# The last token block in three stores, and one batch's input loads ten steps later

## The chip, the cores and the metric

The kernel runs on one core of a Trainium2 chip. Its time is device microseconds, the median of several executions. A profile of one execution is read beside it: busy times of the engines, waits between them, DMA transfers. The engines are named as there: PE is TensorE (matmuls; PEld its weight loads), ACT is ScalarE, DVE is VectorE, POOL is GpSimd, and SP is the engine that issues most DMAs.

## The reference, cut to what matters

```python
X = np.fft.rfft(x, axis=1)                  # x: 8 x 3008 x 256
y = np.fft.irfft(X * (filt_r + 1j * filt_i)[None], n=3008, axis=1)
h = y.reshape(24064, 256) @ w_in            # 256 x 2048
g = h / (1 + np.exp(-beta * h))             # beta: one value per column
out = g @ w_out                             # 2048 x 256, float32
```

A filter over the sequence in the frequency domain, and then two dense layers with a Swish between them.

## The kernel before, in words

**The two halves.** The transform of one batch is cut into four stages of small matmuls: s1 (line 572), s2 (588, followed by the filter's multiplications on VectorE and one addition, yh, on POOL, 607), s3 (617) and s4 (639). Between s1 and s2, and between s3 and s4, the data goes through DRAM to be rearranged: stores `d<-a` and loads `a<-d` (lines 352 and 580, called a2 loads here), stores `d<-z` and loads `zz<-d` (623 and 628). The input rows come by `load_x`, four DMAs of 384 KB per batch, which POOL issues (line 171)[...].

The dense layers go over 47 blocks of 512 tokens, each in 16 steps, one per 128 columns of the hidden layer; 752 steps in all. In step s two matmuls per piece of tokens put the hidden columns into `hps` (line 726), a PSUM tile with two buffers. ScalarE reads it, applies the Swish and writes `gT` (line 735), 128 x 512 in bfloat16. Two steps later, four matmuls (line 746) multiply it with `wout_sb` and add to `acc`, one matmul for each group of 128 tokens. `acc` is two PSUM tiles per block, each of two groups, out of a pool of three. After step 16 of a block both are copied to `ost` and stored.

**What sets the order.** The program's order is written out by hand, and each engine runs its instructions in that order. Batch 0 is transformed ahead of the steps, with all engines. Batch b's transform is spread over the steps in which batch b-1's tokens go through the dense layers: `at(step, function, ...)` puts a piece of work into a table `plan`, and each step runs, in this order, its two hidden matmuls and Swish, the pieces that the table has for it, and the four output matmuls of two steps before. For batch 1, whose base step is 0, s1 is at steps 0 to 7, the a2 loads at step 10, s2 at steps 19 to 46 and s3 five steps after each s2; the second batch's (index 1) z stores follow every third s3. s1 of the third batch (index 2) starts at step 54. The four x loads of the third batch are at steps 14, 17, 20 and 23; POOL issues them between its other work, SP issues the a2 loads, z stores and output stores.

**The end.** The last block is handled like the others, but its two `acc` tiles are copied by ScalarE and VectorE at once, and stored by two DMAs of SP, 256 KB each (line 762); other blocks are copied by VectorE twice and stored by one DMA of 512 KB (line 764).

Of the kernel before, what the change touches and what calls it, by code (L numbers as in the profile page):

```python
# [10 lines left out]
P = 128  # L11
# [4 lines left out]
F32 = mybir.dt.float32  # L16
# [20 lines left out]
def kernel(  # L37
# [10 lines left out]
    nc = tc.nc  # L48

    B, S, D = x.shape  # L50
# [6 lines left out]
    NFB = FF // P  # L57
    NP = 2 * N1
    KP = 4 * NK
    TB = 512  # L60
    assert TOK % TB == 0
    NBLK = TOK // TB
    NSTEP = NBLK * NFB
# [7 lines left out]
    tw = dict(reuse_waits="tile")  # L71
# [31 lines left out]
    wout_sb = wpool.tile([P, NFB, D], BF16, name="wout_sb", tag="wout_sb")  # L103
# [6 lines left out]
    def evac(dst, src, on_act, scale=None):  # L110
        if on_act:
            nc.scalar.activation(dst, src, ACT.Copy, scale=1.0 if scale is None else scale)  # L112
        elif scale is None:
            nc.vector.tensor_copy(dst, src)  # L114
        else:
            nc.vector.tensor_scalar_mul(dst, src, scale)  # L116
# [439 lines left out]
    hpsum = ctx.enter_context(tc.tile_pool(name="hpsum", bufs=2, space=bass.MemoryType.PSUM, **tw))  # L556
    opsum = ctx.enter_context(tc.tile_pool(name="opsum", bufs=3, space=bass.MemoryType.PSUM, **tw))
    fpsum = ctx.enter_context(tc.tile_pool(name="fpsum", bufs=3, space=bass.MemoryType.PSUM, **tw))
    gpool = ctx.enter_context(tc.tile_pool(name="gpool", bufs=4, **tw))
    a2pool = ctx.enter_context(tc.tile_pool(name="a2pool", bufs=5, **tw))  # L560
    zpool = ctx.enter_context(tc.tile_pool(name="zpool", bufs=2, **tw))
    zzpool = ctx.enter_context(tc.tile_pool(name="zzpool", bufs=4, **tw))
# [2 lines left out]
    ostp = ctx.enter_context(tc.tile_pool(name="ostp", bufs=2, **tw))  # L565
# [86 lines left out]
    def at(s, fn, *a):  # L652
        plan.setdefault(int(s), []).append((fn, a))

    def s1_steps(b, units_, steps, act, on_act=()):
        assert len(steps) == len(units_)
        for i, s in zip(units_, steps):
            at(s, s1, b, i, i in on_act)
            if i % 4 == 3:
                at(s, a1_store, b, i // 4)  # L660

    def s23_steps(b, steps, lag, act):
        assert len(steps) == NU
        for i, s in enumerate(steps):
            at(s, s2, b, i)
            at(s + lag, s3, b, i, i % act == act - 1 if act else False)

    def s4_steps(b, steps, act):
        assert len(steps) == J // 4 * NDC
        for i, s in enumerate(steps):  # L670
            at(s, s4, b, i, i % act == act - 1 if act else False)

    for b in range(1, B):
        o = first_step[b - 1]
        if b == 1:
            s1_steps(1, range(16), [o + i // 2 for i in range(16)], False, range(1, 16, 2))
            for g in range(NG):
                at(o + 10, a2_load, 1, g)
            s23_steps(1, [o + r for r in (19, 21, 23, 26, 28, 30, 34, 36, 39, 41, 44, 46)], 5, 1)
            for h in range(J // JG):  # L680
                at(o + 56, zz_load, 1, h)
            s4_steps(1, [o + 67 + (i * 12) // 15 for i in range(16)], 2)
            for f in (2, 3):
                at(f, load_wout, f * WG)
                at(f, scale_wout, f * WG)
            if B > 2:
                for g in range(4):
                    at(o + 14 + 3 * g, load_x, 2, g)
                late = (54, 55, 56, 57, 58, 59, 60, 61, 66, 67, 68, 70, 72, 73, 74, 76)
                s1_steps(2, range(16), [o + r for r in late], False)  # L690
                for g in range(NG):
                    at(o + 80, a2_load, 2, g)
                if B > 3:
                    for g in range(4):
                        at(o + (62, 68, 88, 92)[g], load_x, 3, g)
            continue
        base = [o + 16 * n + s for n in range(4) for s in (4, 8, 12)]
        if b == 2:
            base[:6] = [o + r for r in (8, 12, 19, 22, 26, 29)]
        s23_steps(b, base, 6, False)  # L700
        for h in range(J // JG):
            at(o + 70, zz_load, b, h)
        s4_steps(b, [o + 80 + (i * 13) // 15 for i in range(16)], False)
        if b + 1 < B:
            early = [o + 16 * n + s for n in range(4) for s in (7, 13)]
            late = [o + s for s in (66, 67, 69, 70, 72, 73, 75, 76)]
            s1_steps(b + 1, range(16), early + late, False)
            for g in range(NG):
                at(o + 82, a2_load, b + 1, g)
            if b + 2 < B:  # L710
                for g in range(4):
                    at(o + (30, 62, 88, 92)[g], load_x, b + 2, g)

    blk = {}
    LAG = 2
    for s in range(NSTEP + LAG):
        if s < NSTEP:
            i, fb = divmod(s, NFB)
            t0 = i * TB
            hps = hpsum.tile([P, TB], F32, name="hps", tag="hps")  # L720
            pos = t0
            while pos < t0 + TB:
                b, n0 = divmod(pos, S)
                ln = min(S - n0, t0 + TB - pos)
                for dc in range(NDC):
                    nc.tensor.matmul(  # L726
                        hps[:, pos - t0 : pos - t0 + ln],
                        lhsT=win_sb[:, dc, fb * P : (fb + 1) * P],
                        rhs=ys[b][:, dc, n0 : n0 + ln],
                        start=(dc == 0),  # L730
                        stop=(dc == NDC - 1),
                    )
                pos += ln
            gT = gpool.tile([P, TB], BF16, name="gT", tag="gT")
            nc.scalar.activation(gT[:], hps[:], ACT.Silu, scale=beta_sb[:, fb : fb + 1])  # L735
            blk[s] = gT
        for fn, a in plan.get(s, ()):
            fn(*a)
        if s >= LAG:
            i, fb = divmod(s - LAG, NFB)  # L740
            t0 = i * TB
            gT = blk.pop(s - LAG)
            if fb == 0:
                acc = [opsum.tile([P, 2, D], F32, name="acc", tag="acc") for _ in range(2)]
            for tb in range(4):
                nc.tensor.matmul(  # L746
                    acc[tb // 2][:, tb % 2, :],
                    lhsT=gT[:, tb * P : (tb + 1) * P],
                    rhs=wout_sb[:, fb, :],
                    start=(fb == 0 and tb % 2 == 0),  # L750
                    stop=(fb == NFB - 1),
                    skip_group_check=True,
                )
            if fb == NFB - 1:
                ost = ostp.tile([P, 4, D], F32, name="ost", tag="ost")
                rows = out[t0 : t0 + TB, :].rearrange("(c p) d -> p c d", p=P)
                last = s == NSTEP + LAG - 1
                for h in range(2):
                    hs = slice(2 * h, 2 * h + 2)
                    evac(ost[:, hs, :], acc[h][:], last and h == 0)  # L760
                    if last:
                        nc.sync.dma_start(rows[:, hs, :], ost[:, hs, :])
                if not last:
                    nc.sync.dma_start(rows, ost[:])


# [1 line left out]
_INS = ['x', 'filt_r', 'filt_i', 'moe_w_in', 'moe_w_out', 'moe_beta']  # L768
_OUTS = [((24064, 256), 'float32')]
# [25 lines left out]
```

## Time and profile before

| what | value |
|---|---|
| median of 5 runs (785.72 to 787.02) | 786.1 us |
| the profiled execution | 786.1 us |
| its span, first to last instruction | 784.0 us |
| TensorE busy | 764.6 us |
| ScalarE busy | 559.3 us |
| VectorE busy | 437.9 us |
| POOL busy | 151.4 us |
| mean granted TensorE clock | 0.998 |
| output stores of the last block: issue to landing, least and most | 2.1 and 2.4 us |
| a2 loads: least, median and most | 3.1, 5.1 and 9.7 us |

Times within the span count from its first instruction. A row of the timeline gives the start, the duration, the engine, the line and operation, what is written and read, and in brackets how long the engine stood idle before it and what released it. Matmuls are pipelined: one of 256 columns shows 0.27 us, but they follow each other every 0.108, so starts are compared, not durations. The chain is the work that ended last, followed back from the last instruction to whatever released each piece.

### The profile page before, as it was taken

Reading aid. Unit: us, or ns where it says so; the run is one execution under the profiler, and the core shown is the slowest. Engines: PE = TensorE matmul, PEld = TensorE weight load, DVE = VectorE, ACT = ScalarE, POOL = GpSimd, SP = SyncE. Lnnn points to the kernel's source line nnn. Section 1 sums busy time; section 2 is a strip of 40 time slices with the busy share of each in tenths; the row PEclk is TensorE's granted clock in tenths of the full one; section 3 lists DMA queues with packets and bytes.
Section 4 is the critical chain, followed back from the end, with each engine's and each line's share of the span. In section 5 each row is a group of like instructions: output and inputs, shape, how many; then the busy total and the mean of one; then the engine's idle time right before and its main releaser. Section 6 shows DMA issues by size and latency. Waiting matters only on the chain.

```text
span 784.0 us, 15166 instructions
## 1 busy us (share of the span) xinstructions
PE 764.6 (98%) x5978; PEld 545.0 (70%) x6071; DVE 437.9 (56%) x681; ACT 559.3 (71%) x824; POOL 151.4 (19%) x160
## 2 busy tenths in 40 slices
PE   8799999999999999999999999999999999999997
PEld 5666667766677667866678666776667766676664
DVE  8747754776556665566656675566655666321001
ACT  7787867676677766777667766677766777777775
POOL 6724300322012120122101222012200222000000
PEclk9999999999999999999999999999999999999999
DMA  9968385234922349133580416612164111500101
GB/s 175 227 184 189 101 205 166 68 88 120 240 72 65 98 114 255 35 85 98 122 235 29 130 52 166 190 65 79 48 188 127 55 48 48 155 28 28 55 28 55
DMA packets 89819, 88.51 MB, mean 113 GB/s; under 512 B 5692, under 2 KB 80956, under 8 KB 89748
## 3 DMA queue, kind: packets, MB, share of 16 engines
q1 hardware_dynamic: 85716, 73.94, 31.9%
q0 software_dynamic: 4032, 13.60, 10.3%
q8 instruction: 47, 0.77, 0.4%
q14 instruction: 24, 0.20, 0.1%
HBM read 54.47 MB, written 46.66 MB: 129 GB/s over the span
## 4 chain that ended last, share of the span: by engine, by line
PE 94%; ACT 3%; DVE 1%; issue 1%; DMA 1%; POOL 0%; POOLq 0%; ACTq 0%
PE acc L746 43%; PE hps L726 39%; PE ps L572 3%; PE ps L639 3%; PE ps L617 3%; PE ps L588 2%; DMA a<-d 1%; ACT zT L112 1%; ACT zz L112 1%; ACT aT L112 0%; ACT t3s L291 0%; DVE y L116 0%; PE sps L396 0%; PE sps L444 0%; PE tps L396 0%
## 5 line engine op out<-in xcount | busy, mean ns | idle before, releaser
L735 ACT ACTIVATE gT<-hps,beta_sb 128x512 bf16<-128x512 f32 x752 | 516.7, 687 | 208.7 <-PE hps L726 188.6
L746 PE MATMUL acc<-wout_sb,gT 128*128 128x256 bf16 x3008 | 453.3, 272 | 2.5
L726 PE MATMUL hps<-y,win_sb 128*128 128x512 bf16 (+7 forms) x1636 | 428.3, 350 | 1.1 <-ACT y L112 0.6
L746 PEld LDWEIGHTS <-gT 128*128 128x128 bf16 x3008 | 287.5, 98 | 126.2 <-issue 1.2
L607 POOL TENSOR_TENSOR yh<-a_t,b_t 128x512 bf16<-128x512 f32 x84 | 106.4, 1266 | 420.7 <-DVE b_t L606 419.9
L726 PEld LDWEIGHTS <-win_sb 128*128 128x128 bf16 x1728 | 164.8, 98 | 25.5 <-issue 0.7
L114 DVE COPY ost<-acc 128x512 f32<-128x512 f32 x93 | 59.9, 685 | 147.6 <-PE acc L746 147.6
L114 DVE CAST a<-ps 96x512 bf16<-96x512 f32 x104 | 70.9, 685 | 52.1 <-PE ps L572 48.0
L602 DVE TENSOR_TENSOR a_t<-ps,fr_sb 128x512 f32<-128x512 f32 x84 | 58.1, 692 | 70.5 <-PE ps L588 70.0
L116 DVE TENSOR_SCALAR y<-ps 128x376 bf16<-128x376 f32 x104 | 56.0, 548 | 59.3 <-PE ps L639 59.1
L603 DVE SCALAR_TENSOR_TENSOR b_t<-ps,fi_sb 64x512 f32<-64x512 f32 x84 | 58.2, 693 | 1.1
L606 DVE TENSOR_TENSOR b_t<-ps,fi_sb 64x512 f32<-64x512 f32 x84 | 57.4, 683 | 1.1
L114 DVE CAST z<-ps 128x512 bf16<-128x512 f32 x72 | 49.3, 684 | 1.7 <-PE ps L617 0.8
L639 PEld LDWEIGHTS <-zz 96*128 96x128 bf16 x448 | 29.8, 98 | 22.9
L572 PE MATMUL ps<-xg,t 94*96 94x512 bf16 x112 | 41.5, 381 | 0.6
L639 PE MATMUL ps<-t,zz 96*128 96x94 bf16 x448 | 34.7, 205 | 0.8
L617 PE MATMUL ps<-yh,t 128*128 128x256 bf16 x168 | 32.1, 273 | 0.6
L588 PE MATMUL ps<-a,t 128*128 128x256 bf16 x168 | 32.1, 273 | 0.6 <-DMA a<-d 0.4
L617 PEld LDWEIGHTS <-t 128*128 128x128 bf16 x168 | 16.2, 98 | 17.7
L588 PEld LDWEIGHTS <-t 128*128 128x128 bf16 x168 | 16.1, 98 | 15.7 <-issue 0.6
L171 POOL DMA_DIRECT2D xg<-in_x_dram x24 | 12.4, 519 | 56.5 <-PE ps L572 56.5
L572 PEld LDWEIGHTS <-t 94*96 94x96 bf16 x112 | 13.8, 123 | 10.4
(103 smaller groups left out, 186.0 us busy)
## 6 DMA issues: line engine op xcount, KB each, us to landing
out_dram<-ost SPq DMA_DIRECT2D x46, 512.0 KB, 3.0
d<-a SPq DMA_DIRECT2D x28, 384.0 KB, 4.6
a<-d SPq DMA_DIRECT2D x28, 384.0 KB, 5.1
d<-z SPq DMA_DIRECT2D x28, 384.0 KB, 3.7
zz<-d SPq DMA_DIRECT2D x28, 384.0 KB, 6.2
xg<-in_x_dram POOLq DMA_DIRECT2D x24, 384.0 KB, 6.6
ws<-in_moe_w_out_dram SPq DMA_DIRECT2D x4, 512.0 KB, 5.9
fr_sb<-in_filt_r_dram SPq DMA_DIRECT2D x12, 128.0 KB, 4.8
```

The lines of the kernel that those rows point to most:

```text
L114: nc.vector.tensor_copy(dst, src)
L572: nc.tensor.matmul(ps[:KP], lhsT=t1[:], rhs=xg[b, g][:NP, jj : jj + 2, :], start=True, stop=True)
L588: nc.tensor.matmul(ps[:, e, :], lhsT=t2[:, k0 + e, :], rhs=st["a2", b, g][:, kk + e, :], start=True, stop=True,)
L602: nc.vector.tensor_tensor(a_t[:], ps[:], fr_sb[:, ks, :], ALU.mult)
L603: nc.vector.scalar_tensor_tensor(b_t[:M], ps[M:], -1.0, fi_sb[M:, ks, :], ALU.mult, ALU.mult)
L606: nc.vector.tensor_tensor(b_t[M:], ps[:M], fi_sb[M:, ks, :], ALU.mult)
L607: nc.gpsimd.tensor_tensor(yh[:], a_t[:], b_t[:], ALU.add)
L617: nc.tensor.matmul(ps[:, e, :], lhsT=t3[:, 2 * i + e, :], rhs=yh[:, e, :], start=True, stop=True)
L639: nc.tensor.matmul(ps[:, e, :NP], lhsT=zz[:, j0 % JG + e, dc * P : (dc + 1) * P], rhs=t4[:], start=True, stop=True,)
L726: nc.tensor.matmul(hps[:, pos - t0 : pos - t0 + ln], lhsT=win_sb[:, dc, fb * P : (fb + 1) * P], rhs=ys[b][:, dc, n0 : n0 + ln], start=(dc ...
L735: nc.scalar.activation(gT[:], hps[:], ACT.Silu, scale=beta_sb[:, fb : fb + 1])
L746: nc.tensor.matmul(acc[tb // 2][:, tb % 2, :], lhsT=gT[:, tb * P : (tb + 1) * P], rhs=wout_sb[:, fb, :], start=(fb == 0 and tb % 2 == 0), ...
```

## The change

Four things differ. The x loads of the third batch go from steps 14, 17, 20, 23 to 24, 27, 30, 33. In the last block the four token groups lag by different numbers of steps behind the Swish: groups 0 and 1 by two as before, group 2 by five and group 3 by seven, each with a bound so that what is left of a group is done together after the last step: groups 0 and 1 end in step 753, group 2 in step 754, group 3 in step 755. Groups 2 and 3 have an `acc` tile each, of which half is used, so that the last block takes three tiles. Groups 0 and 1 are copied together by ScalarE and stored by SP (256 KB); group 2 is copied by VectorE and its store (128 KB) is issued by ScalarE; group 3 is copied by VectorE and stored by SP (128 KB). Since a gT now lives up to seven steps, its pool has nine buffers instead of four. Other blocks keep lag, order, copies and stores.

```diff
-    gpool = ctx.enter_context(tc.tile_pool(name="gpool", bufs=4, **tw))
+    gpool = ctx.enter_context(tc.tile_pool(name="gpool", bufs=9, **tw))
...
                 for g in range(4):
-                    at(o + 14 + 3 * g, load_x, 2, g)
+                    at(o + 24 + 3 * g, load_x, 2, g)
...
-    LAG = 2
-    for s in range(NSTEP + LAG):
+    acc = {}
+    lags = {i: (2, 2, 2, 2) for i in range(NBLK)}
+    lags[NBLK - 1] = (2, 2, 5, 7)
+    outs = {}
+    for s in range(NSTEP):
+        i, fb = divmod(s, NFB)
+        for tb, lag in enumerate(lags[i]):
+            outs.setdefault(min(s + lag, NSTEP + max(1, tb)), []).append((i, fb, tb))
+
+    def acc_of(i, tb):
+        h = tb if i == NBLK - 1 and tb == 3 else tb // 2
+        if (i, h) not in acc:
+            acc[i, h] = opsum.tile([P, 2, D], F32, name="acc", tag="acc")
+        return acc[i, h]
...
+    def out_last(i, tb, ost):
+        rows = out[i * TB : (i + 1) * TB, :].rearrange("(c p) d -> p c d", p=P)
+        if tb == 1:
+            evac(ost[:, :2, :], acc[i, 0][:], True)
+            nc.sync.dma_start(rows[:, :2, :], ost[:, :2, :])
+        elif tb > 1:
+            evac(ost[:, tb, :], acc_of(i, tb)[:, tb % 2, :], False)
+            (nc.scalar if tb == 2 else nc.sync).dma_start(rows[:, tb, :], ost[:, tb, :])
+
+    for s in range(NSTEP + 4):
...
-        if s >= LAG:
...
-            for tb in range(4):
-                nc.tensor.matmul(
-                    acc[tb // 2][:, tb % 2, :],
-                    lhsT=gT[:, tb * P : (tb + 1) * P],
...
+        last = NBLK - 1
+        if s == NSTEP - 1:
+            ost = ostp.tile([P, 4, D], F32, name="ost", tag="ost")
+        for i, fb, tb in outs.get(s, ()):
+            lone = i == last and tb > 1
+            nc.tensor.matmul(
+                acc_of(i, tb)[:, tb % 2, :],
+                lhsT=blk[i * NFB + fb][:, tb * P : (tb + 1) * P],
+                rhs=wout_sb[:, fb, :],
+                start=(fb == 0 and (tb % 2 == 0 or lone)),
+                stop=(fb == NFB - 1),
+                skip_group_check=True,
+            )
             if fb == NFB - 1:
...
+                if i == last:
+                    out_last(i, tb, ost)
+                elif tb == 3:
+                    out_block(i)
```

More of the change, by code (lines that the diff above doesn't have):

```diff
@@ L714, with out_block @@
     blk = {}
-    LAG = 2
-    for s in range(NSTEP + LAG):
+    acc = {}
[11 more added lines that the diff above has]
+        return acc[i, h]
+    def out_block(i):
+        ost = ostp.tile([P, 4, D], F32, name="ost", tag="ost")
+        rows = out[i * TB : (i + 1) * TB, :].rearrange("(c p) d -> p c d", p=P)
+        for h in range(2):
+            evac(ost[:, 2 * h : 2 * h + 2, :], acc[i, h][:], False)
+        nc.sync.dma_start(rows, ost[:])
+    def out_last(i, tb, ost):
+        rows = out[i * TB : (i + 1) * TB, :].rearrange("(c p) d -> p c d", p=P)
+        if tb == 1:
[5 more added lines that the diff above has]
+    for s in range(NSTEP + 4):
         if s < NSTEP:
@@ L738 @@
             fn(*a)
-        if s >= LAG:
[L740 to L744, printed above, removed]
-            for tb in range(4):
-                nc.tensor.matmul(
-                    acc[tb // 2][:, tb % 2, :],
-                    lhsT=gT[:, tb * P : (tb + 1) * P],
[L749 to L753, printed above, removed]
-            if fb == NFB - 1:
[L755 to L764, printed above, removed]
+        last = NBLK - 1
+        if s == NSTEP - 1:
+            ost = ostp.tile([P, 4, D], F32, name="ost", tag="ost")
+        for i, fb, tb in outs.get(s, ()):
[8 more added lines that the diff above has]
+            )
+            if fb == NFB - 1:
+                if i == last:
+                    out_last(i, tb, ost)
+                elif tb == 3:
+                    out_block(i)
 _INS = ['x', 'filt_r', 'filt_i', 'moe_w_in', 'moe_w_out', 'moe_beta']
```

## The prediction

> **What bounds the kernel now.** I read the page's engine table first, then its chain, then the chain of waits for TensorE alone, and then the timeline at two places: around step 19, where the chain leaves TensorE for a DMA, and at the end, where the change works.
>
> ```profile
> span 784.0 us, 15166 instructions
> PE 764.6 (98%) x5978; PEld 545.0 (70%) x6071; DVE 437.9 (56%) x681; ACT 559.3 (71%) x824; POOL 151.4 (19%) x160
> PE 94%; ACT 3%; DVE 1%; issue 1%; DMA 1%; POOL 0%; POOLq 0%; ACTq 0%
> ```
>
> TensorE is busy for 98% of the span and carries 94% of the chain that ended last. So time is won or lost only where TensorE stands still, or after its last matmul. A busy PE alone would not prove that; the start-to-start times in the timeline do: matmuls of 256 columns follow each other every 0.108 us, those of 512 every 0.215, so a full step of the expert part (two and four of them) takes 0.87 us, without gaps.
>
> One gap is in the chain. The lines are the timeline around step 19, and the answer for the a2 loads (line 580):
>
> ```profile
> 55.36 1.05 POOL L171 DMA_DIRECT2D xg<-in_x_dram  x2
> 55.54 4.75 SPq L580 DMA_DIRECT2D a<-d  x4
> 61.27 0.59 PE L726 MATMUL hps<-y,win_sb 128*128 128x512 bf16 x2
> 62.22 0.38 PE L588 MATMUL ps<-a,t 128*128 128x256 bf16 x2 [0.36 <-DMA a<-d]
> ```
>
> Two of the x loads that the change moves are issued at 55.36 and 55.91, the first a2 load at 55.54, so they share the DMA engines. The first a2 load lands 6.6 us after its issue, at 62.2, and step 19 waits for it. The hps matmuls that began at 61.27 had been fed by 61.27 + 2 x 0.215 = 61.70, and the next began at 62.22: TensorE lost **0.52 us** (the row's 0.36 counts from the modelled end of the last matmul).
>
> The end:
>
> ```profile
> 777.14 0.59 PE L726 MATMUL hps<-y,win_sb 128*128 128x512 bf16 x2
> 777.36 0.97 PEld L746 LDWEIGHTS <-gT 128*128 128x128 bf16 x8
> 777.83 0.69 ACT L735 ACTIVATE gT<-hps,beta_sb 128x512 bf16<-128x512 f32 x1 [0.18 <-PE hps L726]
> 778.57 0.33 PEld L746 LDWEIGHTS <-gT 128*128 128x128 bf16 x4 [0.24 <-ACT gT L735]
> 779.01 0.60 ACT L112 ACTIVATE ost<-acc 128x512 f32<-128x512 f32 x1 [0.48 <-PE acc L746]
> 779.23 0.69 DVE L114 COPY ost<-acc 128x512 f32<-128x512 f32 x1 [12.17 <-PE acc L746]
> 779.63 0.88 SPq L762 DMA_DIRECT2D out_dram<-ost  x2
> ```
>
> After the last hps pair TensorE does eight acc matmuls, waits for the last gT (0.69 after the pair's start ScalarE begins, 0.69 later it is done), and does the last four. Then come two copies side by side, and two stores of 256 KB, issued at 779.63 and 780.09, which land after 2.1 and 2.4 us (least and most in the answer for out_dram): at 781.8 and 782.5. From there to 784.0 are 1.5 us of closing. The profiled execution took 786.1 us, its span 784.0, so 2.1 lie around it; 786.1 is also the median, so differences carry over.
>
> **The change, part by part.**
>
> *1. The x loads ten steps later.* Four DMAs of 384 KB and their four POOL instructions of 0.53 us leave steps 14 to 23 and go to 24 to 33. With them gone, the first four a2 loads have the DMA engines to themselves. Two later batches have just that case, loads issued at 127.08 and 211.90 with no x load beside them; the first landed after 3.4 us. So here 55.54 + 3.4 = 58.9, 2.8 us before TensorE wants it: the 0.52 us goes whole. Had the x loads little part in the delay, the gain could be 0; it can't exceed 0.64, the row of the weight load (0.64 idle before the same L588). I take **-0.52**. Nothing downstream waits for a DMA on TensorE (0.4 us in the whole run, this one), so the gain lasts.
>
> What is late next? On POOL the loads now stand between the yh additions, 1.27 us each. In the after kernel's instruction order one comes after the third yh (which ends at 70.33; the next starts at 72.14 in the old trace), one after the fourth (73.42 to 74.31), two after the sixth (77.71 to 80.78). The gaps of 1.8, 0.9 and 3.1 us hold 0.53, 0.53 and 1.06. The wait of the load, for x's old buffer, was over when batch 1's first stage ended at step 7. Behind POOL's yh waits s3, five steps (about 5 us) later. The x rows themselves are needed from step 54 (after 98 us), and land by about 85.
> The Trainium skill speaks against putting loads from POOL there ("SBUF — State Buffer", section on its two sides): while VectorE runs certain fast copies, POOL can't write the descriptors of its DMAs. The rows: loads issued at 66.03 and 70.28, with VectorE at work on stage 2, took 0.53 us to issue and landed after 4.8 and 4.4, against 5.1 for the one at 55.36 with VectorE idle. No lockout is seen here; by the rule a load could wait for a VectorE operation of 0.69, which 13 us of slack swallow. Both give 0.
> On SP's queue and the DMA engines, the moved 1.5 MB meet the z stores issued at 72.80 and 80.19 (384 KB) and an output store at 78.51. In the old trace the first landed after 3.0 with the tail of one x load beside it, the second after 2.8. With more of that company I give them the 6.6 us that the a2 load took in that company: landings at 79.4 and 86.8. ScalarE wants the two z buffers back at steps 39 (83.49 in the old trace) and 46 (some seven steps, about 6 us, later). Slack 4 and 3 us: **0**.
>
> *2. Fewer acc matmuls early in the last block.* Groups 2 and 3 now lag five and seven steps. So steps 738 to 742 have 2, 2, 2, 3, 3 acc matmuls instead of 4: 8 x 0.108 = 0.87 us less. Not all of it is won: hps has two buffers, and the pair of step s+2 must wait until ScalarE has read that of step s: 0.69 + 0.69 + 0.05 (778.52 to 778.57 in the last lines) = 1.43 us per two steps, against 2 x 0.65 = 1.30 of matmuls at six a step. Walking the steps with that bound: step 738 starts at 0, 739 at 0.65, 740 at 1.43 (not 1.30), 741 at 2.08, 742 at 2.86, 743 at 3.62, instead of 5 x 0.87 = 4.34. That is **-0.72**. The two-buffer bound takes 0.15 of the 0.87. Also, group 2's first matmul no longer meets the previous block's copy on VectorE (at 766.4, a step 0.08 longer than its neighbours): -0.08. The last hps pair starts 0.80 earlier, at 776.34 on the old clock, and is fed at 776.77.
>
> *3. The same matmuls at the end.* TensorE now has 20 acc matmuls behind that pair instead of 12: 2.17 us, to 778.94, with no wait: the last gT is ready at 776.34 + 1.43 = 777.77, and ten matmuls fill the time to 777.86. Before, the feed ended at 779.02 (last start 778.915). So TensorE's end is level (-0.08); the gap of 0.13 us before the last four is filled, and that is about what the two-buffer bound cost. What moves is the first copy: groups 0 and 1 are complete after 12 of the 20, at 778.07.
>
> *4. Copies and stores.* ScalarE's copy starts 0.22 after the last feed, as it did (778.79 to 779.01), so at 778.29, takes 0.60, and SP issues 256 KB at about **778.92**, 0.71 earlier. Group 2 is fed at 778.51, VectorE copies 256 columns from 778.73. No such row exists in the trace; by 685 ns for 512 columns and 548 for 376 it is 1.0 ns a column, so 0.43 (0.34 if half of 0.69). ScalarE issues the store at 779.18. Group 3: fed 778.94, copied 779.17 to 779.60, SP issues at 779.62. In the DMA view of this stretch bytes move from 0.8 us after the first issue, at 310 to 390 GB/s, and the 512 KB take 1.6 us; a landing comes about 0.4 after the last byte. Now: first byte 779.72, no hole (the second store's bytes can start at 780.0, the third's at 780.4, while the first's move until 780.5), last byte 781.3, landing 781.7 to 781.8. Against 782.5: **-0.7 to -0.8; I take -0.72.**
> Here the Trainium skill again speaks against the change ("DMA: Bandwidth & Descriptors", its anatomy of one DMA and the part on issuing engines): a DMA costs about 2.0 us fixed plus bytes at 436 GB/s whatever its size, and issuing from several engines saves issue time alone. By that the last 128 KB land at 779.62 + 2.0 + 0.3 = 781.9: a gain of 0.6. By the trace's own 256 KB row (2.1 landing, so 1.3 fixed and 0.8 moving), one of 128 KB alone would land after 1.7, at 781.3: a gain of 1.2. The shared engines' queue gives 0.7 between them, and that I keep. ScalarE's queue has issued no DMA in this trace, so its cost is open: from -0.1 (the 0.4 us of SP issue saved, half of it useful) to +0.3 if closing waits longer for one more queue.
>
> *5. gpool with nine buffers instead of four:* more SBUF, no instruction. The gT activations still wait for hps alone; in the instruction order the first a2 load takes over waits for setup loads that the second had, all long over: 0.
>
> Sum: -0.52 - 0.72 = -1.24, so 782.8 for the span and **784.9 us** (-0.16%).
>
> **Rivals.** (a) *More than that*: the last small store lands nearly alone (-1.2), the step-19 gap counts 0.64: 784.3, with run-to-run noise to 784.0. For it: the first 256 KB store landed in 2.1. Against: 512 KB have to move behind the first issue, at the rate seen.
> (b) *One half fails*: the closing absorbs the tail (ScalarE's store is late, or SP's closing waits on it) and only -0.5 is left, 785.6; or the a2 load is late for another reason and only the tail remains, 785.4. For the first: the unknown queue. Against the second: the landings of 3.4 us without x loads.
> (c) *Slower*: the moved x loads delay the z store of 72.80 until after 83.49. ScalarE's queue is in order, so the z copy holds up gT behind it, and after two steps TensorE. It decides once that store takes over 10.7 us; the worst landing of any a2 load, four deep beside x loads, was 9.7. If it took 13.5, 2.8 us are lost, some 0.8 of which (one pair ahead) TensorE covers: 784.9 + 2.0 = 786.9. To be over +0.2% it needs a store of about 14.3 us.
>
> **How the numbers follow.** A measurement of this kernel tells some 0.2% (1.57 us) from no change: the five runs go from 785.72 to 787.02. My forecast 0.58 (own range 784.5 to 785.3), (a) 0.20, (b) 0.15, (c) 0.07. Faster by over 0.2% means under 784.53: most of (a) and the low edge of the forecast, 0.23. Slower by over 0.2% (above 787.67): a part of (c), with what I haven't thought of, 0.06. Between: 0.71. The range 784.1 to 785.8 leaves out the end of (a), (c), and a corner of (b).
>
> **What would show it.** Right: no wait for a<-d at step 19, and the first a2 load landing 3.4 after issue; three steps near 766 that ScalarE paces at 0.71; no gap in the last 20 acc matmuls; three stores issued near 778.4, 778.7 and 779.1 (0.52 before the times of part 4, by the front's gain), the last landing near 781.2, span 782.8. Wrong: a wait of ScalarE's z copies for d<-z between 83 and 92; x loads that hold up yh; a store from ScalarE that lands last; a closing longer than 1.5 us.

## The result, and the profile after

The changed kernel takes 784.71 us (median; 784.21 to 785.69) against 786.43 for the kernel before, measured beside it. The ratio, by the means, is 0.9979, 95% interval 0.9974 to 0.9985: 0.21% less, 1.65 us, with an interval of 1.2 to 2.0. The forecast was 784.9, 1.24 us less. Where a difference is small, means over all executions are used below: 786.39 for the kernel before (the 116 executions on four chips that ran beside the experiments, standard deviation 0.69), 784.80 for the changed one (26, deviation 0.44). A mean of the kernel before differs by up to 0.4 us from chip to chip, so a difference of a few tenths between runs on different chips is not safe.

The profiled execution took 784.39 us, its span 782.6. From its page, span, busy times and chain by engine:

```profile
span 782.6 us, 15166 instructions
PE 763.8 (98%) x5978; PEld 544.7 (70%) x6071; DVE 438.0 (56%) x682; ACT 558.5 (71%) x824; POOL 151.6 (19%) x160
PE 95%; ACT 3%; DVE 1%; issue 1%; POOL 0%; POOLq 0%; ACTq 0%
```

TensorE is still busy for 98%, and the DMA share of the chain is gone. The timeline of the changed kernel around step 19:

```profile
55.70 2.18 SPq L580 DMA_DIRECT2D a<-d  x4
61.46 0.31 PEld L588 LDWEIGHTS <-t 128*128 128x128 bf16 x2
61.67 0.38 PE L588 MATMUL ps<-a,t 128*128 128x256 bf16 x2
```

The duration in the first row is that of the four issues, not of the transfers. No x load stands before the a2 loads; the first lands after 3.2 us, at 58.9, and s2's matmuls follow without a wait. Against the old trace the start of step 20's Swish, counted from that of step 0, is 20.39 us instead of 20.91: the 0.52 is gained. The end of the changed kernel, in the timeline:

```profile
765.95 4.30 ACT L765 ACTIVATE gT<-hps,beta_sb 128x512 bf16<-128x512 f32 x6 [0.18 <-PE hps L756]
766.33 0.38 PE L774 MATMUL acc<-wout_sb,gT 128*128 128x256 bf16 x2
766.68 0.59 PE L756 MATMUL hps<-y,win_sb 128*128 128x512 bf16 x2
...
775.81 0.59 PE L756 MATMUL hps<-y,win_sb 128*128 128x512 bf16 x2
776.25 2.35 PE L774 MATMUL acc<-wout_sb,gT 128*128 128x256 bf16 x20
776.51 0.69 ACT L765 ACTIVATE gT<-hps,beta_sb 128x512 bf16<-128x512 f32 x1 [0.18 <-PE hps L756]
777.76 0.60 ACT L112 ACTIVATE ost<-acc 128x512 f32<-128x512 f32 x1 [0.56 <-PE acc L774]
778.19 0.86 DVE L114 COPY ost<-acc 128x256 f32<-128x256 f32 x2 [11.67 <-PE acc L774]
778.38 0.37 SPq L741 DMA_DIRECT2D out_dram<-ost  x1
778.65 0.37 ACTq L744 DMA_DIRECT2D out_dram<-ost  x1
779.08 0.35 SPq L744 DMA_DIRECT2D out_dram<-ost  x1
```

The first line is six Swishes in 4.30 us, 0.72 each: ScalarE works at 0.69 and stands less than 0.1 between them, where other steps leave it 0.18. The two after it show the step in which TensorE waits for an hps buffer: the acc pair that began at 766.33 was fed at 766.55, and the hps pair starts at 766.68, 0.13 later. Then 20 acc matmuls in one row, and three stores at 778.38, 778.65 and 779.08, landing 2.2, 2.3 and 2.2 us later. The last lands at 781.3, before 782.5.

### The profile page after: what moved, and what is told of

Read it like the earlier page. It is cut to its first block, busy times and chain, and to the rows that moved or that the text cites. A ratio compares the mean times of both kernels' runs of the same rounds, so it can differ in the third digit from the quotient of the medians.

```text
span 782.6 us, 15166 instructions
## 1 busy us (share of the span) xinstructions
PE 763.8 (98%) x5978; PEld 544.7 (70%) x6071; DVE 438.0 (56%) x682; ACT 558.5 (71%) x824; POOL 151.6 (19%) x160
## 4 chain that ended last, share of the span: by engine, by line
PE 95%; ACT 3%; DVE 1%; issue 1%; POOL 0%; POOLq 0%; ACTq 0%
PE acc L774 43%; PE hps L756 39%; PE ps L572 3%; PE ps L639 3%; PE ps L617 3%; PE ps L588 2%; ACT zT L112 1%; ACT zz L112 1%; ACT aT L112 0%; ACT t3s L291 0%; DVE y L116 0%; PE sps L396 0%; PE sps L444 0%; PE tps L396 0%; ACT a L112 0%
## 5 line engine op out<-in xcount | busy, mean ns | idle before, releaser
L114 DVE COPY ost<-acc 128x512 f32<-128x512 f32 (+1 forms) x94 | 60.1, 680 | 147.1 <-PE acc L774 147.1
```

## The experiments

Diffs are against the kernel before where so said, otherwise against the changed kernel.

**1. The x loads alone** (against the kernel before):

```diff
-                    at(o + 14 + 3 * g, load_x, 2, g)
+                    at(o + 24 + 3 * g, load_x, 2, g)
```

> The kernel before with the third batch's x loads at steps 24 to 33, nothing else. Theory: the a2 load of step 10 lands 3.2 to 3.4 us after its issue, the step-19 wait is gone, all starts after it are 0.53 us earlier, the end is as before: 786.4 - 0.5 = 785.9 us. Rival (the shorter a2 landing came from the larger gT pool, which moves buffers and so which earlier loads the a2 load waits for): the landing stays near 6.6, 786.4 us. The x loads may also cost at the z stores: then above 786.4.

Measured: 785.89 us (mean 785.93, deviation 0.34), ratio 0.9995 (0.9987 to 1.0003). The first a2 load lands after 3.3 us with the old pool too, so the larger pool is not what shortened it. The mean falls by 0.46, and the spread halves. In the profile the 20 steps take 20.39 us.

**2. The end alone:**

```diff
-                    at(o + 24 + 3 * g, load_x, 2, g)
+                    at(o + 14 + 3 * g, load_x, 2, g)
```

> The changed kernel with the x loads back at steps 14 to 23. Theory: the step-19 wait is back (0.5 us) and all of the end's gain stays: the last store lands 0.7 us earlier, and what the profile after shows beyond that (1.30 instead of 1.48 us from the last landing to the end of the span, 1.8 instead of 2.1 us around the span) belongs to the end of the kernel: 786.4 - 1.15 = 785.25 us. Rival (that rest is chance or comes from the front): 786.4 - 0.72 = 785.7 us.

Measured: 785.86 us (784.36 to 788.83; mean 786.03, deviation 1.12), ratio 0.9998 (0.9990 to 1.0005). The theory's 785.25 did not hold; the rival's 785.7 lies within the interval. The halves alone give 0.46 and 0.36 in the mean, together 1.59. The profile says where the rest went: the first a2 load lands 7.5 us after its issue, and the 20 steps take 21.92 us. The wait at step 19 cost not 0.5 but 1.5.

**3. Three stores, but all groups at a lag of two:**

```diff
-    lags[NBLK - 1] = (2, 2, 5, 7)
+    lags[NBLK - 1] = (2, 2, 2, 2)
...
-            outs.setdefault(min(s + lag, NSTEP + max(1, tb)), []).append((i, fb, tb))
+            outs.setdefault(min(s + lag, NSTEP + 1), []).append((i, fb, tb))
...
-        h = tb if i == NBLK - 1 and tb == 3 else tb // 2
+        h = tb // 2
...
-            lone = i == last and tb > 1
+            lone = False
```

> The changed kernel with all four groups of the last block at a lag of two, in two acc tiles as in the other blocks, but still copied and stored in three parts (256, 128, 128 KB; ScalarE issues the second). Theory (the lag is what brings the first store forward, the split alone nearly nothing): the first store is issued at the old time less 0.53, all 512 KB move behind it, the last landing 0.1 us earlier than without the split: 786.4 - 0.53 - 0.1 = 785.8 us. Rival (small stores are what pays): the last 128 KB land 1.7 us after an issue near 780.0 - 0.53, 0.8 earlier than the old last landing: 785.1 us.

Measured: 785.51 us (mean 785.61), ratio 0.9989 (0.9981 to 0.9997). From the timeline of its end:

```profile
779.10 0.42 DVE L114 COPY ost<-acc 128x256 f32<-128x256 f32 x1 [12.06 <-PE acc L774]
779.56 0.44 ACTq L744 DMA_DIRECT2D out_dram<-ost  x1
779.58 0.27 PE L774 MATMUL acc<-wout_sb,gT 128*128 128x256 bf16 x1 [0.51 <-DVE ost L114]
779.61 0.37 SPq L741 DMA_DIRECT2D out_dram<-ost  x1
780.34 0.35 SPq L744 DMA_DIRECT2D out_dram<-ost  x1
```

The last landing is at 782.52; the last Swish starts 0.01 us earlier than in the old trace, where the last landing was at 782.53. So nothing lands earlier, and the last small store takes 2.2 us, not 1.7. But this version has a wait of its own, so it does not show what the split alone is worth. Groups 2 and 3 share an `acc` tile here, and group 3's last matmul waits until VectorE has copied group 2: it starts at 779.58, though the matmul before it began at 778.79. Without that wait VectorE could copy group 3 right behind group 2, and the third store would be issued some 0.35 earlier. By this estimate the split alone could land up to 0.3 earlier; no run shows it.

**4. The lags, but two stores:**

```diff
-            (nc.scalar if tb == 2 else nc.sync).dma_start(rows[:, tb, :], ost[:, tb, :])
+        if tb == 3:
+            nc.sync.dma_start(rows[:, 2:, :], ost[:, 2:, :])
```

> The changed kernel with its lags and copies, but groups 2 and 3 in one store of 256 KB from SP after group 3's copy. Theory: bytes move behind the first store for only 0.4 us longer, the last store is issued as in the changed kernel and lands 2.1 to 2.4 us later (2.2 for the 128 KB there): 784.7 + 0.0 to 0.25 us. Rival (the third store must be small): 784.7 + 0.5 us.

Measured: 784.74 us (mean 784.78), ratio 0.9979 (0.9970 to 0.9988): the changed kernel's time. Its last 256 KB land 2.2 us after their issue, as long as the 128 KB of the changed kernel take. Against experiment 3, on the same chip, it is 0.82 faster in the mean, that version's wait included. The cleaner comparison is with experiment 6 below, which has the same buffers, the same x loads and two stores of 256 KB, but a lag of two (and one copy for groups 2 and 3 together). Counted from the first Swish of the steps, the first store of experiment 4 is issued 0.73 us earlier, the second 0.49, and the last landing comes 0.73 earlier (738.63 against 739.36). So the lag is what pays at the end, and the third store adds nothing that shows.

**5. Nine gT buffers alone** (against the kernel before), and **6. with the x loads moved:**

```diff
-    gpool = ctx.enter_context(tc.tile_pool(name="gpool", bufs=4, **tw))
+    gpool = ctx.enter_context(tc.tile_pool(name="gpool", bufs=9, **tw))
```

> The kernel before with nine gT buffers instead of four, nothing else. The two halves alone gave 0.4 (x loads) and 0.45 us (end), together 1.65; the run with the end alone waited 1.4 us at step 19 in its profile, the kernel before 0.52. Theory A (the gT pool moves the a2 buffers, the first a2 load then waits for more earlier loads, starts later against the x loads, and loses to them by more): the wait at step 19 grows, 786.3 + 0.7 = 787.0 us, with runs up to 788.8. Theory B (the wait at step 19 is a race that comes out differently in each execution, whatever the pool): 786.3 us with the spread of the kernel before. The time around the span tells if the 0.3 us that the changed kernel saves there come with the pool (1.8) or not (2.1).

> The kernel before with the moved x loads and nine gT buffers, end unchanged. Without the collision at step 19 the pool can only show in what lies around the span. Theory A: 785.9 - 0.3 = 785.6 us if the 0.3 us around the span come with the pool, with 1.8 us around it. Rival (they come with the code of the end): 785.9 us, with 2.1 around it.

Measured: 786.28 us (785.33 to 790.11; mean 786.44, deviation 1.26), ratio 1.0001 (0.9990 to 1.0011), and 786.01 us (mean 785.97, deviation 0.39), ratio 0.9995 (0.9987 to 1.0004). The time around the span is 1.78 in both, so those 0.3 us come with the buffers and not with the end. Whether they are a gain is open. Experiment 6 takes as long as experiment 1 (785.97 and 785.93), its span being 0.34 longer in the mean; but the two ran on different chips. Experiment 4 ran on the chip of experiment 1 and is 1.14 faster in the mean, and there the profiles need the 0.3: 0.71 in the last landing, counted from the first Swish, 0.08 from there to the end of the span and 0.29 around it make 1.08. With the x loads at their old steps the spread is again large, though the deviation of experiment 5 rests on one execution of 790.11 (0.72 without it). Its profile has an a2 load of 7.3 us.

**7. Group 2's store from SP:**

```diff
-            (nc.scalar if tb == 2 else nc.sync).dma_start(rows[:, tb, :], ost[:, tb, :])
+            nc.sync.dma_start(rows[:, tb, :], ost[:, tb, :])
```

> The changed kernel with group 2's store issued by SP instead of ScalarE. Theory: SP is free when group 2's copy ends (its first issue, 0.37 us, ends near 778.75, the second could begin near 778.8, 0.15 later than from ScalarE), and ends before the third at 779.1, which may slip by 0.1: 784.7 + 0.0 to 0.1 us. Rival (ScalarE's queue costs or saves time in opening or closing): off by 0.2 us or more, either way.

Measured: 784.14 us (784.00 to 784.85, eight executions), ratio 0.9974 (0.9964 to 0.9984), whose interval holds the changed kernel's 0.9979. In the profile the second store is issued 0.47 after the first instead of 0.27, the third 0.98 after it instead of 0.70; the last landing, counted from the Swish of step 743, is the same within 0.02 us. So ScalarE's queue brings the landing no forward. The mean, 784.28, is nevertheless 0.52 under that of the changed kernel (on another chip), and the profile has a reason that is not the queue: from the last landing to the end of the span it has 0.97 us, the changed kernel 1.34. At the end SP goes through a list of waits. In all fourteen profiles it stands still for 0.34 to 0.36 us at the same place, counted in its own instructions. In the others this comes after the last landing; here SP has two instructions more, and the stop falls into the wait for a landing, where it costs nothing. Experiment 4, which has no store from ScalarE either, has the stop behind the landing and 1.41 us. Why SP stands there is not shown.

**8. All x loads at step 33:**

```diff
-                    at(o + 24 + 3 * g, load_x, 2, g)
+                    at(o + 33, load_x, 2, g)
```

> The changed kernel with all four x loads at step 33, issued near 77 to 79, just ahead of the output store at 78.0 and the z store at 79.6. Rival (c) of the prediction made to happen: 1.5 MB of x stand in front, the z store, which landed 7.5 us after its issue beside two x loads, takes about 12 and lands after 90.3, where ScalarE's z copy wants its buffer back; ScalarE stalls, TensorE with it after 0.8 us of cover: 784.7 + 0.5 to 2.5 us. Theory of the slack (loads and stores share the engines, the z store gets through in under 10 us): 784.7 us, no wait of ScalarE.

Measured: 784.79 us (784.36 to 786.60), ratio 0.9985 (0.9977 to 0.9992); beside experiment 7 on the same chip it is 0.65 more, but that one is quicker behind the last landing by 0.36, as just said. The timeline has the wait that rival (c) spoke of:

```profile
76.92 2.05 POOL L171 DMA_DIRECT2D xg<-in_x_dram  x4
77.79 0.38 SPq L735 DMA_DIRECT2D out_dram<-ost  x1
79.47 9.48 SPq L623 DMA_DIRECT2D d<-z  x2
91.19 0.60 ACT L112 ACTIVATE z<-ps 128x512 bf16<-128x512 f32 x1 [0.93 <-DMA d<-z]
```

The third line merges two z stores, at 79.47 and 88.60. The one issued at 79.47 lands 11.6 us later, at 91.1, and ScalarE's copy stands for 0.93 us until then. By step 60 TensorE has lost 0.5. In the changed kernel the same store took 7.6 us and was done 3 us before its buffer was wanted (90.3).

**9. The pool behind the others**, and **10. the end alone once more.** The non-additive halves were still open. Here the end alone (experiment 2) has its nine buffers in two pools, the five new ones behind all others, so that everything else lies as before:

```diff
-    gpool = ctx.enter_context(tc.tile_pool(name="gpool", bufs=9, **tw))
+    gpool = ctx.enter_context(tc.tile_pool(name="gpool", bufs=4, **tw))
...
+    gpool2 = ctx.enter_context(tc.tile_pool(name="gpool2", bufs=5, **tw))
...
-            gT = gpool.tile([P, TB], BF16, name="gT", tag="gT")
+            gT = (gpool if s % 9 < 4 else gpool2).tile([P, TB], BF16, name="gT", tag="gT")
```

> The kernel with the end alone (x loads at steps 14 to 23), its nine gT buffers split: four where the old pool stood, five behind all other pools, so that all other buffers lie where they lay before and the first a2 load waits for its old, shorter list. Open is why end and x loads alone gave 0.33 and 0.43 us in the mean, both 1.56. Theory A (the larger pool, by what the first a2 load waits for, makes the collision at step 19 worse): mean 786.36 - 1.13 = 785.2 us, standard deviation back near 0.7 from 1.1. Theory B (the collision comes out by chance, the place of the pool has no part): as the run with the end alone on the same chip, mean near 786.0, deviation 1.1.

> The kernel with the end alone once more, beside the one with the split pool on the same chip. Theory A: mean near 786.0 us, deviation 1.1, some 0.8 above the split pool. Theory B: the same as the split pool; if both are near 785.2, the first time was an accident of its draw.

Measured: 784.73 us (mean 784.93, deviation 0.51), ratio 0.9982 (0.9973 to 0.9991), and for the repeat 785.14 us (mean 785.33, deviation 1.02), ratio 0.9983 (0.9973 to 0.9994). The timelines at step 19, first the split pool, then the repeat:

```profile
55.33 1.05 POOL L171 DMA_DIRECT2D xg<-in_x_dram  x2
55.42 4.72 SPq L581 DMA_DIRECT2D a<-d  x4
61.65 0.38 PE L589 MATMUL ps<-a,t 128*128 128x256 bf16 x2
```

```profile
55.34 1.05 POOL L171 DMA_DIRECT2D xg<-in_x_dram  x2
55.52 5.18 SPq L580 DMA_DIRECT2D a<-d  x4
63.30 0.38 PE L588 MATMUL ps<-a,t 128*128 128x256 bf16 x2 [1.60 <-DMA a<-d]
```

The same two x loads at the same time, an a2 load 0.1 us apart; one lands after 5.6 us and costs nothing, the other after 7.7 and costs 1.6. In every profile with the x loads at their old steps: 7.5, 7.3 and 7.7 us with nine buffers in place, 6.6 and 5.6 with the old layout. That and the spread (1.12, 1.26, 1.02 against 0.69 and 0.51) speak for theory A. The times do not settle it. The means of this pair are 0.40 apart with a standard error of 0.35, and the repeat's 785.33 is nearer to the 785.2 of theory B than to the 786.0 of theory A: the first draw of the end alone had been a slow one, 0.70 above its repeat. With both draws together (32 executions, mean 785.79) the distance to the split pool is 0.86, with a standard error of 0.26, but over two chips. A further rival was not tested: how long after the first x load the a2 load is issued, 0.09 us with the split pool, 0.18 in the kernel before, 0.18, 0.21 and 0.44 with nine buffers in place. The one at 0.18 landed after 7.7 us, the kernel before's after 6.6, so this delay alone does not order them. Whether the length of the first load's wait list or the place of its buffer does it was not told apart either.

**11. Lags 2, 2, 3, 3 in all other blocks**, a version meant to be faster. At a block's boundary the changed kernel still has a short stop, here in its timeline near 752:

```profile
751.27 1.29 DVE L114 COPY ost<-acc 128x512 f32<-128x512 f32 x2 [12.68 <-PE acc L774]
751.50 0.61 PEld L774 LDWEIGHTS <-gT 128*128 128x128 bf16 x4
751.72 0.68 PE L774 MATMUL acc<-wout_sb,gT 128*128 128x256 bf16 x4
```

Four matmuls take 0.68 instead of the 0.60 of other steps: the third starts at 752.01, 0.19 after the second instead of 0.11, and just after VectorE's first copy ends at 751.96, which empties the tile that it needs.

```diff
-    lags = {i: (2, 2, 2, 2) for i in range(NBLK)}
+    lags = {i: (2, 2, 3, 3) for i in range(NBLK)}
...
-    def out_block(i):
-        ost = ostp.tile([P, 4, D], F32, name="ost", tag="ost")
...
+    def out_block(i, h):
+        if h == 0:
+            osts[i] = ostp.tile([P, 4, D], F32, name="ost", tag="ost")
+        evac(osts[i][:, 2 * h : 2 * h + 2, :], acc[i, h][:], False)
+        if h == 1:
...
-                elif tb == 3:
-                    out_block(i)
+                elif tb % 2:
+                    out_block(i, tb // 2)
```

> The changed kernel with lags 2, 2, 3, 3 in all blocks but the last (there 2, 2, 5, 7 as before), each half of a block's output copied as soon as it is done. At a block's boundary group 2's first matmul waits for VectorE's copy of the half-tile two halves before: in the trace of the changed kernel 20 such gaps of 0.07 to 0.14 us between acc matmuls are recorded, 1.96 us in all. Theory (that wait is all of the gap; a step later the copy is long done): 784.7 - 2.0 = 782.7 us. Rival (the copy placed a step earlier holds up VectorE's other work, or the gaps come from elsewhere): 784.7 us or more.

Measured: 782.47 us (782.45 to 783.28), ratio to the kernel before 0.9949 (0.9936 to 0.9963). Of the gaps none is left; by step 743, in the last block, TensorE is 1.94 us ahead of the changed kernel's trace, for the 1.96 that were expected. The longer lag and the earlier copy of the first half came together, so which of them is needed was not told apart. The same place in its timeline:

```profile
749.41 1.34 DVE L114 COPY ost<-acc 128x512 f32<-128x512 f32 x2 [12.55 <-PE acc L777]
749.43 0.53 PEld L777 LDWEIGHTS <-gT 128*128 128x128 bf16 x4
749.64 0.60 PE L777 MATMUL acc<-wout_sb,gT 128*128 128x256 bf16 x4
```

**12. The last block at 2, 2, 3, 10 as well** (against experiment 11):

```diff
-    gpool = ctx.enter_context(tc.tile_pool(name="gpool", bufs=9, **tw))
+    gpool = ctx.enter_context(tc.tile_pool(name="gpool", bufs=11, **tw))
...
-    lags[NBLK - 1] = (2, 2, 5, 7)
+    lags[NBLK - 1] = (2, 2, 3, 10)
```

> As the run with lags 2, 2, 3, 3, and the last block at 2, 2, 3, 10 with eleven gT buffers: at most one matmul fewer in a step, so that no step falls under the 0.71 us in which ScalarE frees an hps buffer. In the changed kernel 8 matmuls (0.87 us) were deferred and 0.72 won; here the missing 0.15 should come too: 0.15 us under the run with 2, 2, 3, 3, so 782.55 us if that one is at 782.7. Rival (the end is bound by the stores and not by the matmuls): no difference between the two.

Measured: 782.20 us (782.02 to 783.10), ratio 0.9944 (0.9932 to 0.9957). It beats both kernels: by 0.56% the one before, and by 2.5 us in the medians the changed one (on another chip). The first Swish of the steps began at 43.07 in its profile and at 42.62 in that of experiment 11; counted from there its last landing comes 0.25 us earlier (736.47 against 736.72). That is the right sign for the expected 0.15, but the intervals of the two times lie over each other. In its timeline the stores are at 776.64, 776.70 and 777.46:

```profile
776.02 0.60 ACT L112 ACTIVATE ost<-acc 128x512 f32<-128x512 f32 x1 [0.56 <-PE acc L777]
776.24 0.42 DVE L114 COPY ost<-acc 128x256 f32<-128x256 f32 x1 [11.14 <-PE acc L777]
776.64 0.37 SPq L744 DMA_DIRECT2D out_dram<-ost  x1
776.70 0.37 ACTq L747 DMA_DIRECT2D out_dram<-ost  x1
777.46 0.35 SPq L747 DMA_DIRECT2D out_dram<-ost  x1
```

## Why the prediction was right, point by point

**Part 1, the x loads.** The profile bears the numbers out: 0.52 us, a landing after 3.2 for the 3.4 expected. As an account of all executions it was too simple, and so was the bound of 0.64, which came from one row. The step-19 wait is a race, and one profile is one outcome of it: 0.52 in the old trace, 0 to 1.8 in five profiles with the loads at their old steps. In the mean the move is worth 0.46 in the old layout. On POOL all went as said: the loads at 69.72, 72.81 and 77.10 stand in the gaps, no yh is late, and each took 0.51 to 0.55 us to issue, with no lockout to be seen. The z stores landed after 3.1 and 7.6 us where 6.6 was allowed, the second 1.0 over; its buffer was wanted 3.1 us later still, so nothing waited.

**Part 2, the fewer matmuls.** Right in size: from step 738 to 743 the changed trace gains 0.72 us plus the 0.08 of group 2's old wait (together 0.80 in the starts of the Swish), with six Swishes at 0.72 for the 1.43 per two steps.

**Part 3, the tail of matmuls.** 20 in a row with no gap, as said. The first copy starts at 777.76, on the old clock 778.29 with the front's 0.53 added, for 778.29 forecast.

**Part 4, copies and stores.** Issues forecast at 778.4, 778.7 and 779.1 came at 778.38, 778.65 and 779.08; the copy of 256 columns took 0.425 us for 0.43; the last landing came at 781.28 for 781.2. The reason given, that the bytes behind the first issue set the end, is borne out twice. Between experiments 6 and 4 the last landing moves with the first issue (0.73) and not with the last (0.49). In experiment 7 the third store, issued 0.28 later after the first than in the changed kernel, lands at the same time. The fixed cost plus bytes from the Trainium skill ("DMA: Bandwidth & Descriptors", its anatomy of one DMA) is fitted to DMAs that GpSimd issues, and these stores come from SP and ScalarE, so the 2.3 us that it gives for 128 KB are an estimate at most. The last store took 2.2 us in the changed kernel and 1.9 in experiment 7, not one fixed cost. The 1.7 from the 256 KB row for a store alone is untested: no run here has a store of 128 KB alone.

**Part 5, the pool,** came out at nothing, as said, but partly by luck: "more SBUF, no instruction ... 0" holds only beside the moved x loads. There it shows no change (experiments 1 and 6: 785.93 and 785.97). With the x loads at their old steps the profiles with the larger pool in place lose 1.2 to 1.8 us at step 19, against 0 and 0.52 without. So the move seems to be worth more in the changed kernel than in the kernel before, 1.0 (784.80 against 785.79) for 0.46, though that difference is only two standard errors. Measured alone, the halves sum to 1.06 with both draws of the end, not to the 1.6 of the two together; the plain sum of the forecast came out because the two were made together. That the first a2 load takes over more waits was seen and set to nothing, since they were long over; whether they are the cause stays open.

**The size.** 1.24 us were forecast, 1.65 measured, with 1.24 at the interval's edge. The time, 784.71, lies within the range of 784.5 to 785.3; as a difference 1.65 is just past the range's 1.6, and the 0.21% fall by a hair into the "faster by over 0.2%" that was given 0.23. For the last landing the sum was exact: it comes 1.25 earlier (782.53 to 781.28). What it lacked lies behind. From the last landing to the end of the span the changed kernel has 1.34 us for 1.48, and around the span 1.8 for 2.1. With these the two profiles' difference of 1.71 is accounted for. The prediction had carried both over as they were. Profiles with nine buffers in place have 1.40 or 1.41 with two stores, lagged or not, and 1.33 or 1.34 with three (0.97 in experiment 7); with the pool split it is 1.44. Whether the 0.3 around the span is gained or given back inside it is open (experiment 6). Rival (a), a store landing nearly alone, reaches a similar total by a way that the landings rule out. Rival (b) is out: both halves act. Rival (c) exists (experiment 8) but costs little, since a wait of 0.93 on ScalarE reached TensorE as 0.5; in the changed kernel no z store came near the time at which its buffer was wanted.

## What to carry to other kernels

When the engine that bounds a kernel is never idle, the order of its last pieces still decides when the first output may leave; take deferrable work from early steps into the wait for the last activation, but not more per step than the double buffer allows. Small gaps at block boundaries, 20 of about 0.1 us recorded here, can be worth more than the whole tail (1.9 us for 0.7); a further step of lag for half of the groups, with the first half copied at once, removed them. When two versions are compared, ask whether the edit has brought in a wait of its own (experiment 3), or moved one out of sight (experiment 7). A wait behind contending DMAs, as at step 19 here, can be a race: look at several executions and at the spread of times before the size in one profile is believed, and give two halves of a change that share a buffer layout a joint run.

## What was not expected of the hardware

Five things. The time around the span fell from 2.1 to 1.8 us with nine gT buffers for four, whatever the end looked like and also with the pool split in two. SP stands still for 0.34 to 0.36 us at one place in its instructions, in all fourteen profiles, and whether that costs anything depends on what it falls behind. The first a2 load beside the same two x loads, issued within 0.5 us of each other, landed after 5.6 to 7.7 us, and after 3.2 to 3.4 without them. The start of the first Swish lay between 42.45 and 43.26 us in fourteen profiles, a deviation of 0.28, near the 0.3 to 0.4 that remains in the times of the kernels without the wait at step 19 or that of experiment 8; it may be the greater part of that. And a store of 128 KB behind 256 KB of another took no less time to land (2.2 to 2.3 us, 1.9 and 2.1 in experiment 7) than most of those of 256 KB (2.1 to 2.4).
